# A planned attention kernel: a new order of its first quarter, half of that quarter of x by transposing DMA, and new lengths in its planner

## The chip, the cores and the metric

The kernel runs on one core of a Trainium2 chip. The time is the device time of an execution in microseconds (us), given as a median over several executions. In the lines of the profile PE is TensorE, DVE is VectorE, ACT is ScalarE and POOL is GpSimd; L190 and its like are lines of the kernel. All runs told here are in the fast state. A ratio is the mean time of one kernel's fast runs over the mean time of the other's fast runs of the same rounds, so it is not quite the ratio of the medians that I quote.

## The reference, cut to what matters

Two independent problems A and B are computed and set side by side. Each is sliding window attention over 2048 positions, with 32 heads of 32 columns and a window of 256:

```python
qkv = (x @ wqkv).reshape(B, S, 3, H, Dh)            # S = 2048, D = 1024, bf16
scores = einsum("bhqd,bhkd->bhqk", q, k) * Dh**-0.5
scores = where(mask, scores, -1e9)                  # 0 <= i - j < 256
o = einsum("bhqk,bhkd->bhqd", softmax(scores), v)
out = o.transpose(...).reshape(B, S, D) @ wo
```

## The kernel before

Everything is one program whose order is fixed when it is built. The heads are taken in 16 groups of four. Scores are computed in 180 "sessions" of four blocks of 128 x 128 for four heads. A session is one set of score matmuls, one exponential on ScalarE (128 x 2048) and masks on GpSimd. Between sessions TensorE works on "chains": eight matmuls that sum up one 512-column piece of Q, K, V or the output in a PSUM bank. There are two such banks. A finished chain is evicted by ScalarE or VectorE, and a chain can only start when the chain two before it is evicted.

The planner keeps a model clock for each engine while it emits the program. It picks the eviction engine that will be done sooner by that clock, and it emits VectorE's other work (reciprocals, normalising, sums of masked edges) when the clock says that VectorE is free:

```python
NS_ROW = 420.0        # TensorE time of one session's scores
NS_PV = 52.0
ACT_EXP = 1800.0      # one exponential
COST = {"act": 590.0, "dve": 670.0, "or": 560.0, "rinv": 930.0, "mult": 900.0,
        "edge": 620.0}

class _Clock:
    ...
    def evacuate(self, engines):
        best = min(engines, key=lambda e: max(getattr(self, e), self.pe) + COST[e])
        end = max(getattr(self, best), self.pe + 150.0) + COST[best]
        setattr(self, best, end)
        self.banks.append(end)
        return best
...
    # in session(now), after the score matmuls:
        clock.act = max(clock.act, clock.pe) + ACT_EXP
```

The first quarter of x (512 rows, four row blocks) is needed at once. Its rows are loaded as they are and turned (transposed) by TensorE; all other quarters come through a transposing DMA:

```python
    load_wqk(0, 0, nc.scalar)
    for a in range(QB):                                   # QB = 4 row blocks
        nc.sync.dma_start(out=xrow[a], in_=problems[0][0][a * P:(a + 1) * P, :])
        if a == 1:
            load_wqk(0, 1, nc.sync)
    load_wv(0, 0, CT, nc.sync)
    new_x(0, 1)
    load_x(0, 1)                                          # the second quarter, transposing
    ...
    flip(0); keep_warm(4); flip(1); keep_warm(3)          # flip: 8 turns, 2 copies to xT
    first(0, 0); flip(2); flip(3)                         # Q, blocks 0 and 1
    first(1, 0); first(0, 256); first(1, 256)             # K; then Q and K of blocks 2 and 3
    emit(0, chains[0].size)                               # V of blocks 0 and 1
    for now in range(END):                                # the sessions
        ...
```

## Time and profile before

| | before |
|---|---|
| median time, lowest and highest of 6 runs | 609.85 us, 609.59 and 610.95 |
| span of the profiled run | 607.6 us |
| TensorE, VectorE, ScalarE busy | 98%, 77%, 73% |
| first session starts | 13.83 us |
| evictions on ScalarE, on VectorE | 191, 66 of 257 |

The prediction below shows the main lines.

One sequence matters later: what VectorE does for one normalisation. This is the timeline of VectorE in the kernel before; columns are start, length (us), engine, line, operation, tiles, shapes and count.

```profile
23.20 0.96 DVE L524 RECIPROCAL rinv<-acc 128x128 f32<-128x128 f32 x1 [1.60 <-PE acc L513]
...
24.74 0.42 DVE L531 TENSOR_TENSOR oT<-acc,wide 128x256 bf16<-128x256 f32 x1
25.08 1.30 DVE L481 TENSOR_TENSOR both<-pt 128x512 bf16<-128x512 bf16 x2
```

In the gap stand two shuffles that start at 24.20 and 24.41 and last 0.29 and 0.30 us, so the second starts before the first has ended. The edge sums start at 25.08, before the multiplication of 24.74 has ended (25.16). Reciprocal, shuffles and multiplication hold the engine from 23.20 to 25.08, which is 1.88 us, and the two edge sums take 1.30: together 3.18 us. The place is typical: in the 61 normalisations of this trace that VectorE runs through without a pause, it is 1.86 to 1.91 us from the reciprocal to the instruction behind the multiplication.

### The profile page before, as it was taken

What the parts mean: (1) busy time and instruction counts of PE and PEld (TensorE: products, weight loads), DVE (VectorE), ACT (ScalarE), POOL (GpSimd) and SP (SyncE); (2) the same over time, 40 slices, a digit from 0 to 9 for tenths busy, and PEclk for the clock granted to TensorE, in tenths of its full rate; (3) what the DMA queues carried; (4) which work ended last, traced back from release to release, by engine and by line L of the source; (5) the groups of instructions that cost most, each with busy time, mean ns of one, the idle gap of its engine ahead of it and who ended that gap; (6) DMA issues with size and microseconds to landing.
All of it is one profiled execution on the core that took longest, in us unless ns stands there. A gap on an engine that the chain in (4) does not pass through costs nothing.

```text
span 607.6 us, 28768 instructions
## 1 busy us (share of the span) xinstructions
PE 593.6 (98%) x12786; PEld 344.3 (57%) x12838; DVE 468.4 (77%) x1199; ACT 441.1 (73%) x376; POOL 326.3 (54%) x630
## 2 busy tenths in 40 slices
PE   8999999999999999999999999999999999999996
PEld 6555466656655756564556756655455665545443
DVE  1677889898898898897888887898888887897200
ACT  3778887788888887877778877777776777785332
POOL 0565666665666666556555565555555655554000
PEclk9999999999999999999999999999999999999999
DMA  9833110111015501442111100112021040113222
GB/s 234 182 92 89 37 38 3 38 38 39 3 38 90 114 14 30 82 101 77 38 37 38 38 4 8 33 37 81 2 68 34 4 106 21 55 58 120 72 79 64
DMA packets 86802, 35.47 MB, mean 58 GB/s; under 512 B 65552, under 2 KB 86160, under 8 KB 86672
## 3 DMA queue, kind: packets, MB, share of 16 engines
q1 hardware_dynamic: 85632, 33.31, 22.2%
q8 instruction: 102, 1.67, 1.2%
q10 hardware_dynamic: 1040, 0.26, 0.2%
q14 instruction: 28, 0.23, 0.1%
HBM read 17.83 MB, written 8.39 MB: 43 GB/s over the span
## 4 chain that ended last, share of the span: by engine, by line
PE 96%; ACT 2%; issue 1%; DMA 1%; ACTq 0%
PE pp L176 44%; PE pp L172 28%; PE acc L513 13%; PE st L451 10%; ACT pt L459 1%; DMA oT<-in_A_x_dram 1%; PE acc L582 0%; PE pp L568 0%; ACT kT L190 0%; ACT vt L190 0%; PE st L582 0%; ACT osb L190 0%; PE pp L805 0%; ACTq L190 0%
## 5 line engine op out<-in xcount | busy, mean ns | idle before, releaser
L459 ACT ACTIVATE pt<-st 128x2048 bf16<-128x2048 f32 x180 | 338.0, 1878 | 91.6 <-PE st L451 73.5
L471 POOL TENSOR_SCALAR_AFFINE_SELECT pt<-pt 128x512 bf16<-128x512 bf16 x224 | 154.5, 690 | 145.7 <-ACT pt L459 143.1
L467 POOL TENSOR_SCALAR_AFFINE_SELECT pt<-pt 128x512 bf16<-128x512 bf16 x256 | 179.2, 701 | 85.8 <-ACT pt L459 85.8
L524 DVE RECIPROCAL rinv<-acc 128x128 f32<-128x128 f32 x128 | 122.0, 953 | 57.0 <-PE acc L513 56.4
L176 PE MATMUL pp<-xT,wqk 128*32 128x512 bf16 x2712 | 163.1, 379 | 0.0
L481 DVE TENSOR_TENSOR both<-pt 128x512 bf16<-128x512 bf16 x224 | 137.1, 651 | 0.0
L176 PEld LDWEIGHTS <-wqk 128*32 128x32 bf16 x2712 | 69.3, 97 | 54.2 <-issue 0.4
L172 PE MATMUL pp<-xT,wqk 128*128 128x512 bf16 (+1 forms) x323 | 76.7, 369 | 4.1 <-issue 2.4
L176 PE MATMUL pp<-wv,xT 128*32 128x256 bf16 x2436 | 75.9, 273 | 0.0
L451 PE MATMUL st<-qT,kT 32*128 32x384 bf16 (+2 forms) x1488 | 71.5, 269 | 0.1
L176 PEld LDWEIGHTS <-xT 128*32 128x32 bf16 x2436 | 63.8, 97 | 6.2
L529 DVE STREAM_SHUFFLE wide<-rinv 128x128 f32<-128x128 f32 x256 | 64.6, 298 | 0.0
L513 PE MATMUL acc<-pt,vt 128*32 128x128 bf16 (+1 forms) x2160 | 63.3, 239 | 0.0
L172 PE MATMUL pp<-wo_sb,oT 128*128 128x512 bf16 (+1 forms) x269 | 59.3, 373 | 1.3 <-issue 0.9
L451 PEld LDWEIGHTS <-kT 32*128 32x128 bf16 x1488 | 22.2, 92 | 64.5 <-issue 63.3
L190 ACT CAST osb<-pp 128x512 bf16<-128x512 f32 (+1 forms) x52 | 30.0, 577 | 39.1 <-PE pp L172 24.4
L531 DVE TENSOR_TENSOR oT<-acc,wide 128x256 bf16<-128x256 f32 x128 | 54.3, 425 | 4.4
L176 PE MATMUL pp<-wo_sb,oT 128*32 128x512 bf16 x952 | 55.6, 379 | 0.0
L172 PEld LDWEIGHTS <-wqk 128*128 128x128 bf16 x362 | 33.4, 98 | 37.0 <-issue 6.8
L172 PE MATMUL pp<-wv,xT 128*128 128x256 bf16 x415 | 50.9, 273 | 1.4 <-ACT kT L190 0.6
L513 PEld LDWEIGHTS <-vt 128*32 128x32 bf16 x2160 | 35.9, 96 | 26.4 <-issue 24.1
L172 PEld LDWEIGHTS <-xT 128*128 128x128 bf16 x415 | 38.9, 98 | 12.0 <-issue 6.1
(46 smaller groups left out, 386.5 us busy)
## 6 DMA issues: line engine op xcount, KB each, us to landing
out_dram<-osb SPq DMA_DIRECT2D x63, 128.0 KB, 1.8
wqk<-in_B_wqkv_dram SPq DMA_DIRECT2D x32, 128.0 KB, 2.5
wqk<-in_A_wqkv_dram SPq DMA_DIRECT2D x24, 128.0 KB, 2.7
wo_sb<-in_A_wo_dram SPq DMA_DIRECT2D x16, 128.0 KB, 2.2
wv<-in_B_wqkv_dram SPq DMA_DIRECT2D x16, 128.0 KB, 2.8
wo_sb<-in_B_wo_dram SPq DMA_DIRECT2D x16, 128.0 KB, 2.4
oT<-in_A_x_dram SPq DMA_DIRECT2D x4, 256.0 KB, 5.4
wv<-in_A_wqkv_dram SPq DMA_DIRECT2D x2, 512.0 KB, 5.9
```

Source lines behind the costliest of these rows:

```text
L172: nc.tensor.matmul(out[:, lo:hi], lhsT=lhsT, rhs=rhs, start=start, stop=stop, skip_group_check=True)
L176: nc.tensor.matmul(out[c:c + 32, lo:hi], lhsT=lhsT[:, c:c + 32], rhs=rhs, start=start, stop=stop, tile_position=(0, c), skip_group_check=True)
L190: nc.scalar.copy(out=out, in_=in_)
L451: nc.tensor.matmul(st[:, r, a:b, :], lhsT=kT[32 * r:32 * r + 32, j * P:(j + 1) * P], rhs=qT[32 * r:32 * r + 32, q * P:(q + b - a) * P], st ...
L459: nc.scalar.activation(out=pt[:, :, :n, :].rearrange("p r a q -> p r (a q)"), in_=st[:, :, :n, :].rearrange("p r a q -> p r (a q)"), func= ...
L467: nc.gpsimd.affine_select(out=blk, in_=blk, pattern=[[0, 4], [1, P]], compare_op=ALU.is_ge, fill=0.0, base=0, channel_multiplier=-1)
L471: nc.gpsimd.affine_select(out=blk, in_=blk, pattern=[[0, 4], [-1, P]], compare_op=ALU.is_gt, fill=0.0, base=0, channel_multiplier=1)
L481: nc.vector.tensor_tensor(out=both[:, :, h, :], in0=pts[s0][:, :, a0, :], in1=pts[s1][:, :, a1, :], op=ALU.add)
L513: nc.tensor.matmul(acc[32 * r:32 * r + 32, o:o + w_], lhsT=lhsT, rhs=src[:, r, :, :], start=(x == 0), stop=(x == len(moves) - 1), tile_pos ...
L524: nc.vector.reciprocal(out=rinv[:], in_=acc[:, 2 * P:3 * P])
L529: nc.vector.stream_shuffle(out=wide[:, h * P:(h + 1) * P], in_=rinv[:], mask=[16 * h] * 32)
L531: nc.vector.tensor_tensor(out=oTs[(pi, k)][:, t, (p % 2) * 256:(p % 2 + 1) * 256], in0=acc[:, 0:256], in1=wide[:], op=ALU.mult)
```

## The change

The intent was to fill TensorE better at the start, and to make the model clock follow the trace. Blocks 0 and 1 are turned on TensorE, blocks 2 and 3 come by a transposing DMA (256 rows), V of blocks 0 and 1 is computed between Q/K of blocks 0 and 1 and Q/K of blocks 2 and 3, each sum has its own bank, and the planner's lengths are raised to figures read from a trace.

```diff
-NS_ROW = 420.0
-NS_PV = 52.0
+NS_ROW = 440.0
+NS_PV = 55.0
-ACT_EXP = 1800.0
-COST = {"act": 590.0, "dve": 670.0, "or": 560.0, "rinv": 930.0, "mult": 900.0,
-        "edge": 620.0}
+ACT_EXP = 1900.0
+COST = {"act": 610.0, "dve": 700.0, "or": 570.0, "rinv": 970.0, "mult": 1080.0,
+        "edge": 680.0}
...
-        clock.act = max(clock.act, clock.pe) + ACT_EXP
+        clock.act = max(clock.act, clock.pe + 100.0) + ACT_EXP
...
-    for a in range(QB):
+    for a in range(2):
         nc.sync.dma_start(out=xrow[a], in_=problems[0][0][a * P:(a + 1) * P, :])
-        if a == 1:
+        if a == 0:
             load_wqk(0, 1, nc.sync)
     load_wv(0, 0, CT, nc.sync)
+    load_x(0, 0, 2, 2)
     new_x(0, 1)
     load_x(0, 1)
...
-    keep_warm(4)
+    keep_warm(3)
+    first(0, P)
     flip(1)
     keep_warm(3)
-    first(0, 0)
-    flip(2)
-    flip(3)
-    first(1, 0)
-    first(0, 256)
-    first(1, 256)
+    first(P, 2 * P)
+    emit(0, chains[0].size)
+    first(2 * P, 4 * P)
+    clock.banks = clock.banks[-2:]
     emit(0, chains[0].size)
```

In the new code `first(lo, hi)` does Q and K of these columns; Q's sum stands in a bank of the accumulator pool, K's in the first bank of the projection pool, and the warming matmuls write to the score tile. The last `emit` is now a second V chain, ahead of session 0.

More of the change, by code (lines that the diff above doesn't have):

```diff
@@ L544, in _fast_path @@
     new_wv(0)
-    xrow = [rows[:, 2 * a:2 * a + 2, :].rearrange("p t n -> p (t n)") for a in range(QB)]
+    xrow = [rows[:, 2 * a:2 * a + 2, :].rearrange("p t n -> p (t n)") for a in range(2)]
     load_wqk(0, 0, nc.scalar)
-    for a in range(QB):
+    for a in range(2):
         nc.sync.dma_start(out=xrow[a], in_=problems[0][0][a * P:(a + 1) * P, :])
-        if a == 1:
+        if a == 0:
             load_wqk(0, 1, nc.sync)
     load_wv(0, 0, CT, nc.sync)
+    load_x(0, 0, 2, 2)
     new_x(0, 1)
@@ L562, in _fast_path @@
             load_wv(1, 0, CT, nc.sync)
-    warm = ps_proj.tile([P, 512], F32, name="pp")
+    warm = ps_st.tile([P, 4, SLOTS, P], F32, name="st")[:, 1].rearrange("p a q -> p (a q)")
     def keep_warm(n):
         for _ in range(n):
-            nc.tensor.matmul(warm[:], lhsT=blank[:, 0:P], rhs=blank[:, 0:512], start=True, stop=True)
+            nc.tensor.matmul(warm, lhsT=blank[:, 0:P], rhs=blank[:, 0:512], start=True, stop=True)
     keep_warm(6)
-    flips = [ps_acc.tile([P, 512], F32, name="acc") for _ in range(2)]
-    flips = [f[:] for f in flips]
-    flips.append(ps_st.tile([P, 4, SLOTS, P], F32, name="st")[:, 0].rearrange("p a q -> p (a q)"))
-    flips.append(None)
-    held = [{}, {}]
+    flips = [ps_acc.tile([P, 512], F32, name="acc")[:]]
+    held = [{"pp": ps_acc.tile([P, 512], F32, name="acc")[:]}, {}]
     def flip(a):
-        if a == 3:
-            flips[a] = ps_acc.tile([P, 512], F32, name="acc")[:]
-        f = flips[a].bitcast(BF16).rearrange("p (ct q) -> p ct q", q=P)
+        f = flips[0].bitcast(BF16).rearrange("p (ct q) -> p ct q", q=P)
         for ct in range(CT):
@@ L587, in flip, with first @@
         nc.vector.tensor_copy(out=dst[:, half:, :], in_=f[:, half:, :])
-    def first(which, lo):
-        for _, f in qk_steps(0, which, 0, lo, lo + 256, held[which], last=lo > 0):
-            f()
+    def first(lo, hi):
+        for which in range(2):
+            for _, f in qk_steps(0, which, 0, lo, hi, held[which], last=hi == 512):
+                f()
     flip(0)
-    keep_warm(4)
+    keep_warm(3)
+    first(0, P)
     flip(1)
     keep_warm(3)
-    first(0, 0)
-    flip(2)
-    flip(3)
-    first(1, 0)
-    first(0, 256)
-    first(1, 256)
+    first(P, 2 * P)
+    emit(0, chains[0].size)
+    first(2 * P, 4 * P)
+    clock.banks = clock.banks[-2:]
     emit(0, chains[0].size)
```

## The prediction

> **What bounds the kernel now.** I read the page first (parts 1, 2 and 4), then the stretches of the span, then the waits of TensorE, then the first 14 us instruction by instruction. From the page:
>
> ```profile
> PE 593.6 (98%) x12786; PEld 344.3 (57%) x12838; DVE 468.4 (77%) x1199; ACT 441.1 (73%) x376; POOL 326.3 (54%) x630
> ...
> PEclk9999999999999999999999999999999999999999
> ...
> PE 96%; ACT 2%; issue 1%; DMA 1%; ACTq 0%
> ```
>
> TensorE is busy for 98% and carries 96% of the chain that ended last. A busy PE is not yet a PE at its peak, so I checked it against streaming time. At the end of the kernel ScalarE takes one finished chain of eight 512-column matmuls every 1.73 us, which is 0.216 us a matmul. From the program: QK has 16 groups x 4 quarters x 2 x 8 = 1024 such matmuls, the output projection 512, V 1024 of half the length: 442 us. Scores are 180 sessions at 0.33 us in the chain that ended last (59 us); PV is 16 groups x 76 units of 128 columns (four column groups at once, 0.054 us) = 66 us. Together 567 us of work that the change doesn't touch. The stretches show where the other 40 us can be:
>
> ```profile
> 0.00:7.53 7.53, 5.93 (x29) 2.68 (x30) 0.84 (x6) 2.46 (x3) 0.70 (x6) 1.00 0.83 197
> 7.53:13.90 6.37, 6.34 (x69) 5.54 (x71) 2.12 (x5) 2.25 (x4) 0.00 (x0) 1.00 1.19 273
> 13.90:564.00 550.10, 543.37 (x12469) 317.86 (x12521) 463.58 (x1182) 423.23 (x346) 325.63 (x624) 1.00 0.22 53
> ...
> 602.20:607.60 5.40, 0.00 (x0) 0.00 (x0) 0.00 (x0) 0.37 (x1) 0.00 (x0) 0.86 0.16 43
> ```
>
> The columns are stretch, length, busy time of PE, PEld, DVE, ACT, POOL, granted clock, DMA share and GB/s. About 8.6 us lie ahead of the first session (worked out below) and 5.4 us behind the last matmul. The rest is mostly about 0.08 us at each change between scores and other matmuls, and a few nanoseconds a matmul. What PE really waits for in the middle is small:
>
> ```profile
> PE pp L172 <- issue: 3.5, 22, 0.2
> PE pp L568 <- DVE ones L783: 1.3, 1, 1.3
> PE pp L172 <- ACT vt L190: 1.0, 2, 0.5
> PE pp L172 <- ACT kT L190: 0.6, 2, 0.4
> PE pp L172 <- DVE oT L531: 0.3, 2, 0.2
> ```
>
> The 3.5 us of "issue" come about every 10 us and are one matmul long, in places where fewer matmul records than weight loads exist: I take them for missing records. What stays is 1.0 + 0.6 + 0.3 = 1.9 us: a chain that waits for the eviction of the chain two before. The start, TensorE alone:
>
> ```profile
> 4.34 1.04 PE L582 MATMUL acc<-ident,oT 128*128 128x128 bf16 x8 [0.29 <-DMA oT<-in_A_x_dram]
> 5.17 1.11 PE L568 MATMUL pp<-top 128*128 128x512 bf16 x4
> 6.26 0.62 PE L582 MATMUL acc<-ident,oT 128*128 128x128 bf16 x8
> 6.72 0.81 PE L568 MATMUL pp<-top 128*128 128x512 bf16 x3
> 7.56 1.06 PE L172 MATMUL pp<-xT,wqk 128*128 128x256 bf16 x8
> ...
> 9.35 2.81 PE L172 MATMUL pp<-xT,wqk 128*128 128x256 bf16 x24
> 11.99 1.91 PE L172 MATMUL pp<-wv,xT 128*128 128x256 bf16 x16
> 13.83 0.40 PE L451 MATMUL st<-qT,kT 32*128 32x384 bf16 x8
> ```
>
> Each line is start, time from it to the last end, engine, line, operation. Row block 0 arrives at 4.30, is turned on PE (L582), and its two copies run one behind the other, on ScalarE to 6.01, on VectorE to 6.46; L568 only keeps PE warm. Useful matmuls start at 7.56, the first session at 13.83. By then PE has done 32 + 16 matmuls of 256 columns, at 0.108 us = 5.2 us of lasting work: 13.83 - 5.2 = 8.6 us are lost.
>
> **What the Trainium skill says.** (1) "TensorE: Matmul & The Clock Gate", section "Wait — 56ns, not 53.3ns?": start to start 426.7 ns cold and 215.7 ns warm at 512 columns, 55.6 ns at 128. The trace agrees: the first warming matmuls start 0.43 us apart, the last chains take 0.216 us a matmul, and eight turns take 0.46 us warm. Turns and 128-column matmuls are therefore priced at 0.056 us. (2) "DMA: Bandwidth & Descriptors", section "Latency and other measured facts": a transposing DMA reaches 261 GB/s in a non-contiguous case. Here its 256-byte packets run at about 290 GB/s (the DMA rate between 10 and 13 us, when nothing else is under way), 3.6 us for 512 rows; the trace's number is used. (3) Same page, "Queues, rings and completion order": each DMA engine goes round its queues, so ScalarE's weight load and SyncE's loads share the engines. The trace shows both queues' packets in the same half microseconds between 3 and 5 us. (4) "PSUM — Partial Sum Buffer", "PSUM: the matmul accumulator": a first matmul clears the accumulate bits of a whole bank. The change closes each column piece's sum before the next starts in the same bank, so it stays correct; no run here tests it.
>
> **The change part by part.**
>
> Turns: two fewer on PE, 16 x 0.056 = -0.9 us, one warming matmul fewer, -0.2 us, and four copies fewer on ScalarE and VectorE, off the path. The first two column pieces are 128 wide: 32 x (0.056 - 0.054) = +0.1 us.
>
> DMA. Landing times of before, issue by issue in the trace: x0 4.30, wq 5.44, x1 6.22, wk 7.32, x2 8.00, x3 8.73, wv 10.37, the transposed second quarter 13.95. The engines are full from 4 us on (DMA share 1.19), so landings add up. In the new order x0, wk, x1, wv, half transpose: wk about 6.4 and x1 about 7.2 (they change places), wv about 10.4 - 1.4 = 9.0 (two row blocks fewer), the half transpose 1.8 us later, about 10.6. The second quarter lands near 14.3, the second group's weights near 17.
>
> PE then, with each start the later of its operand and PE itself:
> - turn 0 at 4.34 (as before), three warming matmuls to 6.0;
> - Q of block 0: first half of the sum at 6.05 after ScalarE's copy, second half at 6.5 after VectorE's; K to 7.2;
> - turn 1 at 7.3 (x1; before 6.26), to 7.8, warming to 8.4;
> - copies to 8.6 and 9.05, Q and K of block 1 to 9.75;
> - V of blocks 0 and 1: wv is there at 9.0, 9.75 to 11.5;
> - Q and K of blocks 2 and 3: half transpose there at 10.6, 11.5 to 13.2;
> - a second V chain. The projection pool has two banks. K took the first, V the second, so this V takes K's bank again and must wait for K's eviction. In before that takes about 0.9 us from the last K matmul (ended near 12.0 to the cast's end at 12.78): a new wait of 0.8 us, then 1.73 us: to about 15.8;
> - session 0 at 15.8, with 6.9 us of lasting work: 8.9 us lost, against 8.6.
>
> So the start gives +0.3 us. Without the bank wait it would be -0.5. The removed turns are mostly eaten because block 1 now arrives behind K's weights, and its copies stand bare.
>
> Planner lengths: no instruction becomes shorter. Traced means are 1878 ns for the exponential, 586 and 692 for evictions, 953 for the reciprocal. The new figures follow them, so the choice between ScalarE and VectorE for evictions should hit fewer busy engines. At stake are the 1.9 us above; I take about half, -1.0 us. The larger row and PV lengths move at most about one matmul from a session to the tail, where it takes the same time on PE.
>
> Sum: 609.83 + 0.3 - 1.0 = 609.1 us.
>
> **The rivals.**
> - The second V chain does not wait (another bank, or K evicted sooner): -0.5 - 1.0, 608.3 us. Against it: in before, V started at 11.99, 0.08 us behind the end of the Q cast whose bank it takes (11.91), as rotating banks would have it.
> - The half transpose comes late or holds up the copies of blocks 0 and 1, since it writes the same tile. If copies waited for its landing at 10.6, the start would lose about 4 us: 613 to 614 us. Against it: in before, PE read blocks 0 and 1 of that tile from 9.35 on while copies wrote blocks 2 and 3, so parts of the tile are told apart; nothing shows this for a DMA. About 7%.
> - The new lengths reshuffle evictions for the worse: sessions have 0.28 us or more between the end of one exponential and the next score matmul, so shifts of 0.05 us don't make PE wait each time, but some chains may meet a busy ScalarE. +1 us: 611 us.
> - DVE or ACT becomes the bound: at 77% and 73% no.
>
> **Range and chances.** The parts that can go either way are 0.8 us (bank wait), 1.0 us (planner), and some 0.5 us on landing times; runs of before alone reach 610.95. I take 607.8 to 610.8. Two per cent is 12.2 us, more than all that is lost ahead of the first session, so faster is nearly excluded; slower by 12 us needs a false wait of the whole schedule.
>
> **What would show it.** Turn 1 near 7.3 instead of 6.26; V of block 0 ahead of Q and K of blocks 2 and 3, starting near 9.8 without a wait for wv; a PE gap of about 0.8 us after K's last matmul, ended by K's eviction; session 0 near 15.8; fewer than 1.9 us of PE waits on evictions behind it; PE again at 98%. I am wrong if the half transpose lands after 11.5, if copies wait for it, or if the middle gains or loses over 2 us.

## More of the kernel before

"Before" was measured again in each group of runs: 609.85, 609.62, 610.06 and 610.09 us.

The evictions are counted from the cast instructions of the two engines in the groups of the profile.

## The result, and the profile after

The changed kernel took 614.95 us (614.44 to 615.23, 6 runs) against 609.85 for before; the ratio is 1.008, 95% interval 1.0067 to 1.0093. It is slower by 5.1 us (0.8%), where the prediction said 0.7 us faster. Spans of the profiled runs: 613.0 against 607.6 us.

The page of the changed kernel:

```profile
PE 594.8 (97%) x12725; PEld 344.5 (56%) x12777; DVE 446.8 (73%) x1169; ACT 453.7 (74%) x402; POOL 328.0 (54%) x630
...
PE 91%; ACT 3%; issue 2%; DMA 1%; SPq 1%; DVE 0%; ACTq 0%; DVEq 0%
```

TensorE is still the bound, with 91% of the chain that ended last instead of 96%. Other engines have got into that chain. VectorE has 22 us less to do (468.4 to 446.8) and ScalarE 13 us more (441.1 to 453.7): evictions moved, 219 of 257 are now on ScalarE instead of 191.

TensorE's waits after (engine, line, releaser: us in total, times, longest):

```profile
PE pp L172 <- DMA xT<-in_A_x_dram: 1.4, 1, 1.4
...
PE pp L172 <- ACT vt L190: 1.2, 3, 0.5
PE pp L172 <- ACT kT L190: 1.2, 3, 0.4
PE pp L176 <- DVE unsafe_i L802: 0.7, 1, 0.7
PE pp L172 <- ACT qT L190: 0.4, 1, 0.4
```

There is one wait for a DMA that before did not have, waits for ScalarE's evictions (L190) of 2.8 us instead of 1.6, and a wait for VectorE in the final check, which the program makes on Q and K near its end. The start, TensorE alone:

```profile
12.64 1.04 PE L172 MATMUL pp<-xT,wqk 128*128 128x256 bf16 x8
13.52 1.91 PE L172 MATMUL pp<-wv,xT 128*128 128x256 bf16 x16
15.36 0.40 PE L451 MATMUL st<-qT,kT 32*128 32x384 bf16 x8
17.11 2.55 PE L172 MATMUL pp<-xT,wqk 128*128 128x512 bf16 x10 [1.36 <-DMA xT<-in_A_x_dram]
```

K of blocks 2 and 3 starts at 12.64, the second V chain follows at once at 13.52 (K's cast on ScalarE only starts at 13.72, so the chain did not wait for it), and session 0 starts at 15.36. In before, session 0 started at 13.83 and the same V chain took 1.76 us after it: for equal work 15.59. So the start itself wins 0.2 us in these two traces. That is less than executions of one start differ by, so it isn't shown: in the eight traces with the old start, session 0 begins between 13.49 and 15.27 us (the first row block lands between 3.98 and 4.69). Then TensorE stands for 1.36 us, because the second quarter of x isn't there.

### The profile page after: what moved, and what is told of

It reads as the page before. It is cut to its first block, busy times and chain, and to the rows that moved or that the text cites. A ratio compares the mean times of both kernels' runs of the same rounds, so it can differ in the third digit from the quotient of the medians.

```text
span 613.0 us, 28647 instructions
## 1 busy us (share of the span) xinstructions
PE 594.8 (97%) x12725; PEld 344.5 (56%) x12777; DVE 446.8 (73%) x1169; ACT 453.7 (74%) x402; POOL 328.0 (54%) x630
## 3 DMA queue, kind: packets, MB, share of 16 engines
q8 instruction: 102, 1.67, 1.1%
## 4 chain that ended last, share of the span: by engine, by line
PE 91%; ACT 3%; issue 2%; DMA 1%; SPq 1%; DVE 0%; ACTq 0%; DVEq 0%
PE pp L176 42%; PE pp L172 26%; PE acc L513 13%; PE st L451 10%; ACT pt L459 2%; DMA xT<-in_A_x_dram 1%; SPq L133 1%; ACT kT L190 0%; ACT vt L190 0%; SPq L548 0%; ACT osb L190 0%; ACT qT L190 0%; DVE rinv L524 0%; SPq L154 0%; SPq L145 0%
## 5 line engine op out<-in xcount | busy, mean ns | idle before, releaser
L481 DVE TENSOR_TENSOR both<-pt 128x512 bf16<-128x512 bf16 x224 | 132.5, 631 | 0.0
L172 PE MATMUL pp<-xT,wqk 128*128 128x512 bf16 (+2 forms) x319 | 75.9, 368 | 6.2 <-issue 3.0
L176 PE MATMUL pp<-wv,xT 128*32 128x256 bf16 x2376 | 74.0, 273 | 0.0
L176 PEld LDWEIGHTS <-xT 128*32 128x32 bf16 x2376 | 62.3, 97 | 5.5
L190 ACT CAST osb<-pp 128x512 bf16<-128x512 f32 (+1 forms) x53 | 30.6, 577 | 39.1 <-PE pp L172 23.1
L172 PE MATMUL pp<-wv,xT 128*128 128x256 bf16 x430 | 53.2, 273 | 2.0 <-ACT kT L190 0.8
L172 PEld LDWEIGHTS <-xT 128*128 128x128 bf16 x430 | 40.6, 98 | 12.8 <-issue 6.0
```

What stands on the lines that cost most here:

```text
L172: nc.tensor.matmul(out[:, lo:hi], lhsT=lhsT, rhs=rhs, start=start, stop=stop, skip_group_check=True)
L176: nc.tensor.matmul(out[c:c + 32, lo:hi], lhsT=lhsT[:, c:c + 32], rhs=rhs, start=start, stop=stop, tile_position=(0, c), skip_group_check=True)
L190: nc.scalar.copy(out=out, in_=in_)
L481: nc.vector.tensor_tensor(out=both[:, :, h, :], in0=pts[s0][:, :, a0, :], in1=pts[s1][:, :, a1, :], op=ALU.add)
```

## The experiments

Twelve kernels ran, all with correct results and five rounds each. In the new start's experiments the old lengths are kept, and the other way round.

| run | what it is | us | its before | ratio, 95% interval |
|---|---|---|---|---|
| e1_lengths | old start, new lengths | 613.36 | 609.62 | 1.0058 (1.0044 to 1.0073) |
| e2_start | new start, old lengths | 611.59 | 609.62 | 1.0030 (1.0017 to 1.0043) |
| e3_cost | before, new COST table | 613.85 | 609.62 | 1.0074 (1.0059 to 1.0088) |
| e4_rowpv | before, new row and PV lengths | 609.49 | 609.62 | 0.9994 (0.9981 to 1.0007) |
| e5_mult | before, mult 1080 | 611.43 | 610.06 | 1.0024 (1.0012 to 1.0036) |
| e6_fewer | before, mult 720, long exponential | 610.59 | 610.06 | 1.0016 (1.0001 to 1.0031) |
| e7_fourturn | new start, four blocks turned on TensorE | 610.94 | 610.06 | 1.0018 (1.0005 to 1.0031) |
| e8_split | new start, second quarter's DMA in two | 610.92 | 610.06 | 1.0015 (1.0002 to 1.0028) |
| e9_oldmap | new lengths, before's eviction engines | 611.11 | 610.09 | 1.0023 (1.0009 to 1.0036) |
| e10_newmap | old lengths, the new eviction engines | 612.37 | 610.09 | 1.0037 (1.0022 to 1.0051) |
| e11_fetch | new start, 48 tiny matmuls early | 610.62 | 610.09 | 1.0010 (0.9996 to 1.0025) |
| e12_best | attempt at a better version | 611.62 | 610.09 | 1.0029 (1.0014 to 1.0043) |

**Which half of the change.** e1 is the kernel before with the new constants of the diff above and nothing else; e2 is the changed kernel with the old constants.

> The kernel before with the new planner lengths alone (its old first quarter). Theory: the new lengths send more evictions to ScalarE (219 of 257 instead of 191), where they stand behind exponentials, and TensorE waits for banks; about +3.7 us: 613.5 us, with over 4 us of TensorE waits on ScalarE's evictions and on the final check. Rival (the first quarter does it all): 609.9 us.

> The new first quarter with the old lengths. Theory: +1.2 to 1.5 us, 611.2 us: the first session starts about as early for the same work, but the second quarter of x lands late and TensorE waits about 1.4 us for it after session 0. Rival (the first quarter does it all): 614.9 us.

The lengths cost 3.7 us and the start 2.0. Together that is 5.7, and the whole change cost 5.1; the intervals, some 0.8 us each way, allow for the difference. e1 shows the waits for ScalarE's evictions (2.9 us) and for the final check (0.7 us), together a little less than the 4 us that I expected, and none for x; e2 shows the 1.4 us wait for x. The rival that the start does it all falls, but the start cost more than I expected.

**Which lengths.**

```diff
# e3_cost, on the kernel before
-COST = {"act": 590.0, "dve": 670.0, "or": 560.0, "rinv": 930.0, "mult": 900.0, "edge": 620.0}
+COST = {"act": 610.0, "dve": 700.0, "or": 570.0, "rinv": 970.0, "mult": 1080.0, "edge": 680.0}
# e4_rowpv, on the kernel before
-NS_ROW = 420.0
-NS_PV = 52.0
+NS_ROW = 440.0
+NS_PV = 55.0
# e5_mult, on the kernel before
-"mult": 900.0
+"mult": 1080.0
```

> The kernel before with the new COST table alone (evictions, or, reciprocal, mult, edge). It sends 238 of 257 evictions to ScalarE. Theory: as slow as all the lengths together or slower, 613 to 615 us. Rival (the row and PV lengths that set how much work goes between sessions): 609.9 us.

> The kernel before with NS_ROW 440 and NS_PV 55 alone. Evictions split 192 to 65, nearly as before. Theory: 609.9 us, within 0.5 us of before. Rival (row and PV lengths): 613 us or more.

> The kernel before with mult at 1080 instead of 900 and nothing else. Evictions on ScalarE 214 of 257 (before 191, all new lengths 219). Theory (the overstated VectorE lengths push evictions to ScalarE, mult first of all): most of the loss of the lengths, 611.5 to 613 us. Rival (it is the sum of many small shifts, or the exponential's length): under 610.5 us.

The COST table alone costs 4.2 us. The row and PV lengths, which set how much work goes between sessions, cost nothing. In e3's trace TensorE waits 4.9 us for ScalarE's evictions (V 2.3, K 1.8, Q 0.8), against 1.6 in before. Mult alone, with 214 evictions on ScalarE, costs 1.4 us, just under the lower end of what I expected: it is a part of the loss, but not most of it. The other entries were not run alone.

**What such a wait looks like.** The same place in the program, first after. TensorE, then ScalarE of the changed kernel:

```profile
365.49 0.39 PE L172 MATMUL pp<-wv,xT 128*128 128x256 bf16 x2
365.72 1.89 PE L172 MATMUL pp<-xT,wqk 128*128 128x512 bf16 x7
368.01 0.81 PE L172 MATMUL pp<-xT,wqk 128*128 128x512 bf16 x3 [0.41 <-ACT vt L190]
```

```profile
365.61 1.88 ACT L459 ACTIVATE pt<-st 128x2048 bf16<-128x2048 f32 x1 [0.77 <-PE st L451]
367.38 0.58 ACT L190 CAST vt<-pp 128x512 bf16<-128x512 f32 x1
```

A V chain ends with the two matmuls of 365.49, and its eviction is given to ScalarE, which has just begun an exponential. The cast starts at 367.38. Meanwhile TensorE does the next chain in the other bank in 1.7 us and then needs V's bank: it stands until 368.01. The eight matmuls from 365.72 (one record is missing), at 0.216 us each, are done by 367.45, so 0.56 us are lost. The 0.41 of the line counts from the modelled end of the last matmul (0.38 us long), and so every such wait in the lists costs some 0.16 us more than it says. In the kernel before, TensorE and then VectorE:

```profile
362.88 0.39 PE L172 MATMUL pp<-wv,xT 128*128 128x256 bf16 x2
363.11 2.54 PE L172 MATMUL pp<-xT,wqk 128*128 128x512 bf16 x10
```

```profile
364.02 0.68 DVE L192 CAST vt<-pp 128x512 bf16<-128x512 f32 x1
```

VectorE took V at 364.02, 0.7 us after the chain's end, and TensorE ran on for ten matmuls without a stop.

**Is it the choice of the engine, or VectorE's other work?** The eviction engine was taken out of the clock's hands. Each of the 257 evictions has a name, and a table says where it goes:

```diff
-        best = min(engines, key=lambda e: max(getattr(self, e), self.pe) + COST[e])
+        best = "dve" if key in ON_DVE else "act"
# e9_oldmap: new lengths, ON_DVE = the 66 evictions of before
# e10_newmap: old lengths, ON_DVE = the 38 evictions that the new lengths leave there
```

> Old first quarter, all new lengths, but each of the 257 evictions put on the engine that it had in before (191 on ScalarE, by name). Theory (the lengths cost through the choice of the eviction engine): back to 610 us; up to 611 us if the final check still waits for VectorE as it does with the new lengths. Rival (they cost through the order and timing of VectorE's other work): 612.5 us or more.

> Old first quarter, old lengths, but each eviction put on the engine that the new lengths choose (219 on ScalarE). Theory: the loss comes with the choice, 612 to 613.5 us, TensorE waits for ScalarE's evictions about 3 us in all. Rival: 610 us.

With old lengths and the new choice (e10), 2.3 us are lost; with new lengths and the old choice (e9), 1.0 us. The sum, 3.3, is close to the 3.7 of both. So the choice of engine is the larger part. The smaller part is what else the new lengths do; e9 carries them all, those of the exponential, the rows and PV too, so the 1.0 us are not shown to be the order of VectorE's other work alone. Neither theory was right alone: e9 missed the 610 that I had expected and lies just beyond the 611 that I allowed, but without the wait in the final check that I had named for it. TensorE's waits in e10:

```profile
PE pp L179 <- ACT vt L197: 1.4, 3, 0.5
PE pp L179 <- ACT kT L197: 1.4, 4, 0.4
...
PE pp L179 <- ACT qT L197: 0.6, 2, 0.4
```

That is 3.4 us on ScalarE's evictions, 1.8 more than in before. In e9 only 0.9 us are on ScalarE (0.3 and 0.6), and 0.5 on a Q eviction that VectorE does late.

The traces can also be laid side by side, by the start of each session. From session 0 to the last output matmul e10 loses 2.75 us on before, and it loses 2.67 of them at six of the 180 sessions (0.57, 0.25, 0.57, 0.17, 0.56 and 0.55 us); elsewhere the two keep step. e3 loses 4.6 us at ten sessions. So a few unlucky evictions cost it, not all that moved. Against e4, which has the same new row and PV lengths, e9 loses 1.9 us, a few tenths at each of several sessions and 0.6 at the late Q eviction. At the place shown above, VectorE takes the same V here too, but 1.54 us after the two V matmuls begin (363.23), where before and e4 need 1.14 and 1.13:

```profile
364.77 0.68 DVE L201 CAST vt<-pp 128x512 bf16<-128x512 f32 x1
```

That fits the order of VectorE's work as the second cause; no run changes that order alone.

**The other direction.**

```diff
# e6_fewer, on the kernel before
-"mult": 900.0
+"mult": 720.0
-ACT_EXP = 1800.0
+ACT_EXP = 1900.0
-        clock.act = max(clock.act, clock.pe) + ACT_EXP
+        clock.act = max(clock.act, clock.pe + 100.0) + ACT_EXP
```

> The kernel before moved the other way: mult 720 instead of 900, and the new, longer exponential. Evictions on ScalarE 164 of 257. Theory: TensorE waits less for evictions than in before (under 1.9 us), 608 to 609.5 us. Rival (any change of the lengths disturbs a tuned order): 611 us or more.

This missed: 164 evictions on ScalarE are not better than 191. TensorE's waits for evictions are 1.5 us instead of 1.9, and the time is 0.5 us longer, with an interval that nearly touches 1; it lies between what the theory and the rival said. So it isn't true that every eviction moved to VectorE helps; before's split is near a balance.

**Where the second quarter of x was.** The landing times and packets of the DMAs, one by one in the traces, are in this table (us). "Stragglers" are the last two completion packets of a transfer when they come apart from the others; "fetch" is a single packet of 16,384 bytes on the queue that the page lists as "q8 instruction". The last data are known to about 0.1 us, since packets of the next transfer follow at once.

| transfer, run | last data | stragglers | fetch (start, length) | landed |
|---|---|---|---|---|
| second quarter, before | 13.36 | none | 13.37, 1.48 | 13.95 |
| second quarter, after | 14.86 | 15.88 | 14.74, 1.16 | 17.07 |
| second quarter, e2 | 14.58 | 15.67 | 14.52, 1.16 | 16.85 |
| second quarter, e7 | 13.19 | 14.16 | 13.18, 1.02 | 15.37 |
| half transpose, e11 | 10.53 | 11.51 | 10.59, 0.94 | 12.62 |
| second quarter, e11 | 15.47 | none | (was at 10.59) | 15.99 |
| half transpose, e2 | 10.3 | none | (comes at 14.52) | 11.51 |
| first half of second quarter, e8 | 12.6 | none | 12.34, 1.23 | 14.52 |

Two things make the second quarter late. First, its data end 1.5 us later than in before. I had counted 0.3: 1.8 for the half transpose less 1.5 for the two row blocks. But between two transposing DMAs there is a hole: from 10.5 to 11.5 us only 288 packets move in the changed kernel, where about 1130 move in a full microsecond. Over the whole hole, from 10 to 12 us, 1.05 us of transfer are missing, nearly all of the 1.2 that I had not counted. Second, an instruction fetch takes a DMA engine for 1.2 us just as the transfer ends. Two of the 32 completion packets, so those of one engine of sixteen, come only when it is over (14.74 + 1.16 = 15.90, seen at 15.88 and 15.89), and the landing comes 1.2 us later still. The signals of the sixteen DMA engines agree: fifteen of the second quarter's come from 15.32 to 15.45, the last at 17.07. In e2 and e7 the last is 1.6 us behind the others too; in the eight traces with the old start all sixteen come within 0.3 us. In before the fetch came at the same point, but all completion packets were out by 13.43.

That a fetch is what delays it was a theory after e2. Two runs test the start further, and one tests the fetch:

```diff
# e7_fourturn, on e2: blocks 2 and 3 loaded as rows and turned again, flips 2 and 3 ahead of V
-    load_x(0, 0, 2, 2)
+    for a in range(2, QB):
+        nc.sync.dma_start(out=xrow[a], in_=problems[0][0][a * P:(a + 1) * P, :])
...   (cut: the tiles that rows and turns of blocks 2 and 3 need)
     first(P, 2 * P)
+    flip(2)
+    flip(3)
     emit(0, chains[0].size)
# e8_split, on e2
-    load_x(0, 1)
+    load_x(0, 1, 0, QB, 0, CT // 2)
+    load_x(0, 1, 0, QB, CT // 2, CT)
# e11_fetch, on e2
-    keep_warm(6)
+    keep_warm(3)
+    for _ in range(48):
+        nc.tensor.matmul(warm[:, 0:32], lhsT=blank[:, 0:P], rhs=blank[:, 0:32], start=True, stop=True)
```

> New first quarter with the old lengths, but blocks 2 and 3 turned on TensorE again, with V still between Q and K. Theory (what costs is the late second quarter behind the transposing half): the second quarter lands near 14.0, no TensorE wait for it, two more turns (0.9 us): about 610.3 us. Rival (the new order of Q, K and V or the shared banks cost it): 611.6 us or more.

> New first quarter with the old lengths, the second quarter's transposing DMA split in two halves of the columns. Theory (TensorE waits for the landing of that one DMA): the first half lands near 14, TensorE goes on right after session 0 and waits at most 0.5 us for the second: 610.5 to 611 us. Rival (a third transposing DMA brings another hole and everything lands later): 611.6 us or more.

> New first quarter, old lengths, three of the six first warming matmuls replaced by 48 tiny ones, so that TensorE runs through some 90 more instructions early and an instruction fetch falls due earlier. Theory (the second quarter lands over 2 us behind its last data because an instruction fetch takes one DMA engine just then): it lands within 1 us of its data, near 15.5, TensorE waits under 0.3 us for it, 610.3 us. Rival (it lands late because two transposing DMAs follow each other): still near 16.9, 611.6 us.

In e7 the quarter lands at 15.37, not at 14.0 as I had expected, because a fetch hits it there too. But it has no half transpose ahead of it, TensorE needs it only at 16.36, and there is no wait. In e8 the first half lands at 14.52, TensorE goes on right after session 0, and the second half (16.31) comes when it is wanted: again no wait for x. Both are about 0.9 us slower than before, and e2 was 2.0: the wait for x is worth some 1.1 us.

e11 shifts the fetch. It comes at 10.59 now, at the end of the half transpose, and now it is the half that has stragglers and lands 2.1 us behind its data; the second quarter has none and lands 0.5 us behind its data. TensorE's timeline in e11:

```profile
12.66 1.03 PE L172 MATMUL acc<-xT,wqk 128*128 128x256 bf16 x8 [0.62 <-DMA xT<-in_A_x_dram]
...
16.24 0.40 PE L451 MATMUL st<-qT,kT 32*128 32x384 bf16 x8
16.57 2.55 PE L172 MATMUL pp<-xT,wqk 128*128 128x512 bf16 x11
```

The wait of 1.36 us behind session 0 is gone, and a wait of 0.62 us for the half has come. The wait behind session 0 went with the fetch, so the theory holds for the second quarter. The half is a mixed case: of its sixteen signals ten come from 12.31 to 12.44 and only the last, at 12.62, alone. A half that no fetch hits is late as well when a second transposing DMA follows (1.2 us behind its data in e2). The hole between the transposing DMAs was there in e11 too (the data of the second quarter took from 10.53 to 15.47), and it is longer where a fetch falls into it: 1.4 us of transfer are missing in e11 and 1.5 between the halves in e8, against 0.7 in e2 and 1.05 in the changed kernel.

**A better version?** In before TensorE's waits on ScalarE's evictions are behind four evictions. e12 takes the start of e8, the old lengths, before's table of engines, and moves these four to VectorE:

```diff
# e12_best, on e8_split
-        best = min(engines, key=lambda e: max(getattr(self, e), self.pe) + COST[e])
+        best = "dve" if key in ON_DVE else "act"
# ON_DVE = the 66 evictions of before, and V of (2, 2), (3, 12), (4, 0) and K of (2, 1)
```

> An attempt to beat both: new first quarter with the second quarter's transposing DMA split in two, old lengths, evictions on the engines of before, except the four behind which TensorE waited in before, which go to VectorE. Theory: start -0.2 us, waits on evictions from 1.9 to under 0.5 us: 608.3 us. Rival (VectorE is just as full there): 609.5 to 610.5 us.

It failed: 1.5 us slower than before. Two of the four waits are gone (near 74 and 143 us in before). A third was never tested: at 226.81 in before TensorE waits for a K eviction, and I had moved the V eviction behind it; the K stayed on ScalarE, and its wait of 0.39 us is still there in e12 (at 228.22). At the fourth, V is now on VectorE, and TensorE waits 0.7 us for it instead of 0.5: there VectorE is full too, as the rival said. A new wait of 0.6 us for a normalisation comes near 42 us, behind a K eviction that the table of before puts on VectorE. No kernel here beats before; e4 equals it.

## Why the prediction was wrong

**The step that failed most** is "Planner lengths": "the choice between ScalarE and VectorE for evictions should hit fewer busy engines. At stake are the 1.9 us above; I take about half, -1.0 us." Measured: +3.7 us (e1). The choice did not hit fewer busy engines: 28 more evictions went to ScalarE, and where one stood behind an exponential TensorE waited for its bank (3.4 us of such waits in e10, against 1.6 in before). I took for granted that lengths read from a trace are better lengths, and of mult, which was raised most, I had quoted no traced length at all. A length in a trace runs to the end of an instruction, but the next one can start before that. In the sequence of VectorE shown above, reciprocal to multiplication hold the engine for 1.88 us. The old lengths say 0.93 + 0.90 = 1.83, the new ones 0.97 + 1.08 = 2.05. With two edge sums it is 3.18 measured, 3.07 old and 3.41 new, so the new lengths charge VectorE 7% too much. But they overcharge ScalarE as well. In before, where the next instruction starts before the one ahead of it has ended, it starts 1.77 us after an exponential's start (old 1.80, new 1.90) and 0.48 us after an eviction's on ScalarE (old 0.59, new 0.61), against 0.61 on VectorE (old 0.67, new 0.70). So the overcharge of VectorE alone doesn't explain why the planner turned to ScalarE. What the counts show is that mult alone sends 214 evictions there, the COST table 238, and all lengths together, the longer exponential among them, 219. That the loss comes through the choice of engine is shown for 2.3 us (e10); that it starts with the COST table is shown by e3; which of the lengths are wrong against which is not tested by a run with other figures. The bound of my gain was also wrong: the waits that existed bound what can be won, not what can be lost, and the six of them cost nearer 2.9 than 1.9 us, by the 0.16 us that each line leaves out.

**The landing of the second quarter**: "The second quarter lands near 14.3". It landed at 17.07, and TensorE waited 1.36 us. The landings ahead of it were right: wk 6.61 against about 6.4, x1 7.32 against 7.2 and wv 9.00 against 9.0. Missing were the hole between two transposing DMAs and the fetch. The half transpose also landed later than the 10.6 that I gave: 11.51 in e2, and 11.73 in the changed kernel, where Q of blocks 2 and 3 starts at 11.77. Its data end in time (10.2), the landing comes 1.2 to 1.5 us later. "After 11.5" was one of the signs of being wrong that I had named, and a middle that loses over 2 us another; both came true.

**The bank wait**: "this V takes K's bank again and must wait for K's eviction", 0.8 us. It did not come; V followed K's last matmul at 13.52. The trace doesn't say which bank it got, but the program does, built again from the changed kernel: K has bank 6 and both V chains have bank 7, so the second V waits for the first V's eviction, which was over at 12.38. This rival of mine ("the second V chain does not wait") was right, and in these traces the start was worth -0.2 us up to session 0 for equal work (I had said +0.3, or -0.5 without the bank wait).

**Right**: the turns and their cost, K's weights and block 1 changing places, turn 1 "near 7.3" (7.43), V "near 9.8" (9.84) without a wait for wv, the streaming rates, and that TensorE stays the bound. The rival "The half transpose comes late or holds up the copies of blocks 0 and 1" was half right: the half came late, but TensorE lost at most 0.2 us to it, and it held up no copy (both of block 0 ended by 6.45). The rival "the new lengths reshuffle evictions for the worse" was right in kind; I gave it +1 us, and it was 3.7.

**What stays open**: the 2.0 us of the new start are the wait for x (1.4), less the start (0.5 in e2's trace), and 0.9 us more behind session 0, which e7, e8 and e11 lose alike (0.9, 0.9 and 1.0 us against before, for equal work). The sum is 1.8; the interval covers the rest. Of the 0.9 us, additional waits on evictions at about 67, 85 and 137 us are the larger steps. They seem to come from other chains ending beside the exponentials; e12, with before's engines by name, still has two of them. Which length tips the planner towards ScalarE, and how the rest of the lengths cost 1.0 us in e9, isn't followed up either.

## What to carry to other kernels

In a planner that chooses between engines, durations from a trace are no safe lengths: here the time from an instruction's start to the next one's start was shorter on both engines. A kernel with lengths by that measure was not run, so try it before you trust it, and judge the lengths of both engines together: what matters is which one seems free first. A kernel whose bound engine is 98% busy is balanced in many places, so bound the loss of a reordering separately from the gain. To find where time is lost, lay two traces side by side session by session. And a transfer that lands a microsecond ahead of its use is not safe at the start of a kernel: look at what else uses the same DMA engines when it ends, and give it a smaller first part.

## What the Trainium skill lacked or had wrong

- "Runtime: NRT & Kernel Launch", section "Instruction fetch mechanics", says that instructions come in 16 KiB blocks over the sequencer's own DMA queue and that fetching is mostly hidden. The traces agree on the block (102 packets, 1.67 MB, so 16,384 bytes each). Missing is that such a block holds a DMA engine for 0.9 to 1.6 us (the 102 fetches of before) and can delay another transfer's completion by over a microsecond: the transfers with stragglers landed 2.1 to 2.3 us behind their last data; of those without, the second quarters of before and e11 landed 0.5 to 0.6 us behind theirs.
- "DMA: Bandwidth & Descriptors", section "DMA Transpose (X-bar)", doesn't say that two transposing DMAs behind each other on one queue don't run on without a hole: in the changed kernel 288 packets moved from 10.5 to 11.5 us, after the second had begun, against about 1130 in a full microsecond. It doesn't say either that the first of the two lands late: 1.2 us behind its data in e2.
